# Pooled attention with a mixture of attention experts behind it, on one core: shared output chunks, another emission clock, another order of matmuls

## The chip, the cores and the metric

The kernel runs on one core of one Trainium2 chip. The metric is device time in microseconds (us), the median of several runs; lower is better. All numbers before the prediction come from runs and from one profiled execution of the kernel before the change.

## The reference

Two stages follow each other, in float32.

```python
# q, k, v: (8, 8, 1152, 64); the queries are averaged in pairs to 576
q_pool = q.reshape(B, H, S // 2, 2, D).mean(axis=3)
attn = softmax(q_pool @ k.T / sqrt(D));  x = attn @ v        # 8 heads -> x: (8, 576, 512)

logits = x @ w_gate                    # 4 experts, the best 2 of each token, softmax over those
for e in range(4):
    q, k, v = x @ wq[e], x @ wk[e], x @ wv[e]                # (8, 576, 64)
    a = softmax(causal(q @ k.T / sqrt(64)))
    out += gate[e] * (a @ v @ wo[e])                         # (8, 576, 512)
```

The maxima of the rows are subtracted before the exponential, so they are computed first. Inputs of `q`, `k`, `wq` and `wk` are large enough (x8) that the matmuls of the scores are done in split form, a high part and a low part.

## The kernel before, in words

**Tiles.** Heads go in pairs: 32 pairs, four to a batch, eight batches. A pair has its two heads in the two halves of the 128 partitions. Matmuls come in three shapes. Shape A (`rows2`, line 293) splits the array by rows, one half for each head: scores and the matmuls of the row maxima. Shape B (`cols2`, line 300) splits it by columns: products with `v` and the sums of the softmax's denominators. Shape C (`mm`, line 284) uses the whole array: projections, the output and small ones. PSUM is eight buffers of 512 columns (`gen`).

**Work of a pair.** `f_max` and `f_mxs` compute scores for the maxima, VectorE reduces them (`row_max`, line 540, into `PM`), and the maxima go as rows into `RM`. `f_st` computes the scores again, transposed and in split form (`qh`, `ql`, `kh`, `kl`, and a matmul with `RM` that subtracts the maximum); ACT takes the exponentials into `pt` (eleven buffers); `f_av` multiplies by `v`, and Pool (GpSimd) adds `pt` into `sacc` for the denominators (line 317). `f_xfin` normalises and splits the result into a high and a low part of `x`, in two ranges of queries, 256 and 320 (`g_split`, lines 707 to 716). The splitting of loaded inputs is done beside it: `f_prepq` adds the two halves of the queries on VectorE and forms `ql` (lines 471 and 483, both with two inputs in SBUF), `f_prepk` forms `kl` on Pool.

**Work of a batch's second stage.** Once four pairs are done, `f_qk` and `f_vproj` project `x`, `f_mmax` and `f_mst` do maxima and scores, `f_mask` masks on Pool, `f_mav` multiplies by `v`, and `f_yfin` leaves `y` (two head pairs of experts, high and low part, 576 tokens). `f_out` multiplies by `wo` in chunks of 128 tokens: five to a batch, the last of 64 tokens. A chunk is six matmuls of 512 columns (two pairs of experts; high by high, low by high, high by low), an ACT copy from PSUM and a store. The weights are split in `f_weights` early in the run (line 1084: VectorE subtracts, two inputs in SBUF). The work of a batch's second stage is laid between the pairs of the next.

**What sets the order.** Each piece of work is a generator (`Flow`). An emission loop (lines 1099 to 1120) keeps a clock for each engine (`clk`, `emit`): every emitted instruction adds a cost written in the code, waits in that clock for what it reads and writes, and adds 0.1 and 0.05 or 0.105 us where PE changes shape. The loop picks the next piece by those clocks, by priorities and by a table, `PLAN`, with a row of thirteen numbers for each of the 32 pairs and one for the tail. The numbers say, in order: how long PE may idle for a piece of the shape that it is in, in general, for scores and for products with `v`; how many waiting products make PE prefer shape B on leaving A; how many make it go there at all without a penalty of 3 us (`av_need`); how far the matmuls of the maxima may run ahead of VectorE; and priorities and lags of the maxima and of the second stage. So the costs and the table fix the order in which instructions are written on every engine; on the chip each engine runs its own list in that order, with semaphores between them.

**VectorE beside Pool.** In `dve_tt` (line 312) a cost of n / 960 + 0.069 us is charged for n elements. Only `any_tt`, which `f_prepq` uses, adds `PORT` = 0.38 us for Pool; the weights' subtraction adds nothing.

Of the kernel before, what the change touches and what calls it, by code (L numbers as in the profile page):

```python
# [7 lines left out]
F32 = mybir.dt.float32  # L8
# [41 lines left out]

PORT = 0.38

# [3 lines left out]

PLAN = [
# [33 lines left out]
]  # L91
INF = float("inf")
SEM = {"PE": 0.2, "ACT": 0.2, "DVE": 0.15, "POOL": 0.15, "SP": 0.0, "": 0.0}
# [58 lines left out]
def pooled_attention_then_moe_kernel(ctx: ExitStack, tc: tile.TileContext, qT, kT, vP, wall, wop, out):  # L152
# [80 lines left out]
    r_gs = ring("gs", [128, 2, 5, 4], F32, 2)  # L233
    r_y = ring("y", [128, 2, SQ], F32R, 2)
    r_ob = ring("ob", [128, DM], F32, 2)
# [5 lines left out]

    def emit(eng, cost, R=(), W=(), xfer=0.0, mode="C", late=0.0):
        t = clk[eng]
        if eng == "PE" and mode != cut[0]:

            t += DRAIN
            cost += LOAD[mode]
        for r in R:
            if r.we != eng:
                t = max(t, r.rw + late)  # L250
        for r in W:
            if r.ue != eng:
                t = max(t, r.ru)
        if eng == "PE":
# [12 lines left out]
        for r in W:  # L267
            if done >= r.w:
                r.w, r.we = done, eng
        return e  # L270
# [5 lines left out]

    def pe_cost(n):
        return max(0.11, n * 0.000455 + 0.002)

# [9 lines left out]
    def rows2(o, terms, R, W):  # L289

        for i, (l, r) in enumerate(terms):
            for j in range(2):
                nc.tensor.matmul(o(j), l(HEAD[j]), r(HEAD[j]), start=i == 0, stop=i == len(terms) - 1)  # L293
            n = o(0).shape[-1]
            emit("PE", pe_cost(n), R, W, 0.0, "A")

# [14 lines left out]

    def dve_tt(o, a, b, op, n, R, W, port=0.0):
        nc.vector.tensor_tensor(o, a, b, op=op)  # L313
        emit("DVE", n / 960 + 0.069 + port, R, W)

    def pool_tt(o, a, b, op, n, R, W):
        nc.gpsimd.tensor_tensor(o, a, b, op=op)  # L317
        emit("POOL", n * 0.0023 + 0.15, R, W)

    def any_tt(o, a, b, op, n, R, W):  # L320
        tail = prog["f"] > NP - 0.5
        e = max([clk["POOL"]] + [r.rw for r in R if r.we != "POOL"]) + n * 0.0023 + 0.06
        d = max([clk["DVE"]] + [r.rw for r in R if r.we != "DVE"]) + n / 960 + 0.069
        if e + (EET if tail else EE0 if prog["f"] == 0.0 else EES) < d:
            pool_tt(o, a, b, op, n, R, W)
        else:
            dve_tt(o, a, b, op, n, R, W, PORT)

# [28 lines left out]
    V, X, Y, VG, XR = {}, {}, {}, {}, {}  # L357
    VT, GT, GS, MT, YR = {}, {}, {}, {}, {}
    lows = {}
    prog = {"f": 0.0}  # L360

    def row(i):
        return PLAN[min(int(prog["f"] + 1e-6), NP)][i]

# [61 lines left out]
    def load_first():  # L426
# [7 lines left out]
        for t in range(3):  # L434
            kh = KH[0, t] = r_kh.new()
            act_copy(kh.ap, ks[t].ap, 384, [ks[t]], [kh], False)
            if t < 2:
                n = sl[t].stop - sl[t].start
                dve_tt(q[:, 0, sl[t]], q[:, 0, sl[t]], q[:, 1, sl[t]], ALU.add, n, [qs[t]], [qs[t]], 0.07)
                act_copy(qh[:, sl[t]], q[:, 0, sl[t]], n, [qs[t]], [QP[t]], False)  # L440
# [265 lines left out]

    def g_split(accs, den, n, hi, lo, res):

# [3 lines left out]
        yield lambda: rdy("ACT", den.rw)  # L712
        act_copy(hi, den[:, :n], n, [den], [res])
        yield lambda: rdy("DVE", res.rw)
        dve_tt(lo, den[:, :n], hi.bitcast(F32), ALU.subtract, n, [den, res], [res])
        den.free()

    def f_xfin(p, hf, acc, sacc):
# [5 lines left out]
        qc = slice(q0, q0 + qn)  # L724
        yield from g_split(accs, den, qn, x[:, 0, qc], x[:, 1, qc], xr)
        flag.add(("x", p, hf))
# [76 lines left out]
    def f_vproj(b, pt):  # L803
# [32 lines left out]
        def op(eng, f, *a, n=20, **kw):  # L836
            f(*a, **kw)
            emit(eng, 0.15 + n * 0.0023 if eng == "POOL" else 0.11 if eng == "ACT" else 0.25, [v32], [gate])

# [137 lines left out]
    def f_mask(b, ep, qb, c, pt, f, kn):  # L977
# [3 lines left out]
                                pattern=[[0, 2], [1, kn]], channel_multiplier=-1)  # L981
        emit("POOL", 0.38, [pt], [pt])
        spawn("mav", f_mav(b, ep, qb, c, pt), av_prio)
# [30 lines left out]
    def f_yfin(b, ep, qb, acc, sacc):  # L1014
# [9 lines left out]
        yr.u, yr.ue = y.u, y.ue  # L1024
        qc = slice(q0, q0 + qn)
        yield from g_split(accs, den, qn, y[:, 0, qc], y[:, 1, qc], yr)
        YR[b, ep, qb] = yr
# [10 lines left out]
    def f_out(b, ts, eps):  # L1038
        tail = b == NB - 1
        ro = r_pt if tail else r_ob  # L1040
        for t in ts:
            n = min(128, SQ - 128 * t)
            tk = slice(128 * t, 128 * t + n)
            yr = lambda ep: YR[b, ep, 0 if t < 2 else 1].rw if (b, ep, 0 if t < 2 else 1) in YR else INF
            yield (lambda: max(r_gen.avail(), ro.avail(), yr(eps[0]), 0.0 if tail else yr(eps[1])), "C")
            ps, ob = r_gen.new(), ro.new()
            o = ob.ap.rearrange("p a b -> p (a b)")[:, 0:DM] if tail else ob.ap
            for i, ep in enumerate(eps):
                if i and tail:
                    yield (lambda: yr(ep), "C")  # L1050
                y = Y[b, ep]
                for k, (yi, W) in enumerate(((0, OH), (1, OH), (0, OL))):
                    mm(ps[:n, :], y[:, yi, tk], W[:, ep, :], i + k == 0, i == 1 and k == 2, 0.233,
                       [YR[b, ep, 0 if t < 2 else 1]], [ps])
            m_prog[b] += 1.4
            act_copy(o[:n], ps[:n, :], DM, [ps], [ob])
            ps.free()
            mv(out[b * SQ + 128 * t:b * SQ + 128 * t + n, :], o[:n], [ob], [])
            ob.free()
        if not tail:  # L1060
            for ep in range(2):
# [5 lines left out]
    def f_weights():  # L1067
# [8 lines left out]
        for i, (hi, lo, src, n) in enumerate(parts):  # L1076
# [71 lines left out]
```

## Time and profile before

| what | value |
|---|---|
| median of 3 runs | 1207.52 us (1206.73 to 1207.64) |
| the profiled execution's own time | 1208.1 us |
| its span, first to last instruction | 1206.4 us |
| mean granted clock of TensorE | 0.993 |

How to read the rows below. PE is TensorE's matmuls, PEld its weight loads, DVE VectorE, ACT ScalarE, POOL GpSimd, SP the queue that issues DMAs. A row of groups gives line, engine, operation, output and inputs by the program's names, shapes, the number of instructions, then busy us and mean ns of one. A row of a timeline gives its start in us, its length in us (from the first start to the last end where several are merged, with their number after x), and in brackets the idle time of that engine before it with what ended it. A row of a stretch gives its bounds, its length, the busy time and instructions of PE, PEld, DVE, ACT and POOL, then the granted clock of TensorE (1.00 is 2.4 GHz, 0.50 is 1.2 GHz), the share of the DMA engines and GB/s. Matmuls are pipelined: consecutive ones overlap in the rows, and the pace is the distance of their starts.

### The profile page before, as it was taken

To read this page: it belongs to the slowest core of one execution; us is meant where nothing else is said; L and a number is where in the kernel's file an instruction comes from. 1 tells how busy PE (TensorE), PEld (TensorE's weight loads), DVE (VectorE), ACT (ScalarE), POOL (GpSimd) and SP (SyncE) were. 2 spreads that over 40 slices of the span, in tenths; PEclk is the share of its full clock that TensorE was granted. 3 is DMA by queue.
4 is the path that set the end of the run, shared out by engine and by line. 5 is a ranking of instruction groups with operands and counts; after the bars stand their busy time and mean duration, and the time that the engine had idled before them with its cause. 6 is when DMAs were issued, how large, how long until landed. Compare 5 with 4: busy or idle time off the path is not lost.

```text
span 1206.4 us, 29495 instructions
## 1 busy us (share of the span) xinstructions
PE 1164.3 (97%) x11257; PEld 902.1 (75%) x11257; DVE 861.6 (71%) x2073; ACT 703.5 (58%) x2024; POOL 973.6 (81%) x852
## 2 busy tenths in 40 slices
PE   6999999989999999999999999999999999999998
PEld 5666787767877778777886777877778777877775
DVE  7898667777677857777587776777667776677265
ACT  5656646645466654666646755566646765466534
POOL 4989998957789976999769987699786996889922
PEclk9989999989999999999999999999999999999999
DMA  5232222022210222113011221112311113200001
GB/s 157 74 93 78 67 61 60 9 79 74 61 54 15 82 71 61 54 53 108 16 51 54 63 93 32 42 54 69 98 41 47 35 63 97 60 22 2 20 22 41
DMA packets 40426, 70.32 MB, mean 58 GB/s; under 512 B 4870, under 2 KB 31452, under 8 KB 40284
## 3 DMA queue, kind: packets, MB, share of 16 engines
q1 hardware_dynamic: 40284, 68.43, 18.2%
q8 instruction: 89, 1.46, 0.5%
q14 instruction: 53, 0.43, 0.1%
HBM read 58.73 MB, written 9.44 MB: 57 GB/s over the span
## 4 chain that ended last, share of the span: by engine, by line
PE 78%; POOL 10%; DVE 8%; issue 2%; ACT 1%; DMA 0%; DVEq 0%; SPq 0%; POOLq 0%; ACTq 0%
PE gen L293 34%; PE gen L300 23%; PE gen L284 20%; POOL sacc L317 8%; DVE PM L540 2%; DVE gen L922 1%; DVE ql L313 1%; POOL kl L317 1%; ACT pt L634 1%; DVE gen L702 1%; DVE WL L313 1%; DVE rd L690 1%; DVE gen L313 1%; POOL pt L980 1%; PE gen L590 0%
## 5 line engine op out<-in xcount | busy, mean ns | idle before, releaser
L317 POOL TENSOR_TENSOR sacc<-sacc,pt 128x640 f32<-128x640 f32 (+2 forms) x588 | 828.1, 1414 | 141.1 <-ACT sacc L309 93.0
L540 DVE TENSOR_REDUCE PM<-gen 128x1 f32<-128x384 f32 x864 | 428.6, 549 | 186.2 <-PE gen L293 142.6
L634 ACT ACTIVATE pt<-gen 128x320 f32<-128x320 f32 (+1 forms) x1152 | 380.2, 433 | 150.0 <-PE gen L293 147.9
L300 PE MATMUL gen<-pt,v 128*64 128x320 f32 (+4 forms) x2752 | 356.1, 402 | 3.8 <-DVE MPM L922 2.1
L300 PEld LDWEIGHTS gen<-pt,v 128*64 128x64 f32 (+1 forms) x2752 | 195.7, 137 | 133.4 <-issue 11.5
L293 PE MATMUL gen<-qh,kh 64*128 64x320 f32 (+1 forms) x1152 | 207.3, 314 | 3.6 <-DVE PM L540 2.8
L293 PE MATMUL gen<-qh,kl 64*128 64x320 f32 (+1 forms) x1152 | 194.8, 298 | 0.0
L293 PE MATMUL gen<-ql,kh 64*128 64x320 f32 (+1 forms) x1152 | 190.2, 294 | 0.0
L293 PE MATMUL gen<-RM,ON 64*128 64x320 f32 (+1 forms) x1152 | 190.0, 293 | 0.0
L293 PE MATMUL gen<-kh,qh 64*128 64x384 f32 x768 | 157.2, 373 | 8.4 <-ACT qh L304 7.5
L293 PEld LDWEIGHTS gen<-qh,kh 64*128 64x128 f32 x1152 | 131.1, 187 | 34.2 <-issue 13.5
L293 PEld LDWEIGHTS gen<-RM,ON 64*128 64x128 f32 x1152 | 129.0, 188 | 0.0
L293 PEld LDWEIGHTS gen<-ql,kh 64*128 64x128 f32 x1152 | 128.7, 187 | 0.0
L293 PEld LDWEIGHTS gen<-qh,kl 64*128 64x128 f32 x1152 | 126.6, 187 | 0.0
L293 PEld LDWEIGHTS gen<-kh,qh 64*128 64x128 f32 x768 | 88.1, 188 | 38.6 <-issue 19.3
L284 PE MATMUL gen<-x,WH 128*128 128x320 f32 (+1 forms) x512 | 105.8, 301 | 7.6 <-DVE x L313 7.6
L317 POOL TENSOR_TENSOR kl<-kraw,kh 128x384 fp32r<-128x384 f32 x96 | 97.6, 1031 | 3.2 <-ACT kh L304 2.5
L284 PEld LDWEIGHTS gen<-x,WH 128*128 128x128 f32 x512 | 81.7, 188 | 11.9 <-issue 9.4
L922 DVE CUSTOM_DVE_ANT_0 gen<-gen,mqk 64x288 f32<-64x288 f32 (+4 forms) x160 | 74.4, 504 | 20.0 <-PE gen L293 17.2
L304 ACT CAST x<-gen 128x256 fp32r<-128x256 f32 x64 | 25.9, 404 | 89.5 <-DVE gen L313 89.5
L284 PE MATMUL gen<-x,WL 128*128 128x320 f32 (+1 forms) x256 | 75.5, 295 | 0.0
L962 ACT ACTIVATE pt<-gen 128x320 f32<-128x320 f32 (+2 forms) x224 | 63.7, 381 | 14.0 <-PE gen L293 12.8
(109 smaller groups left out, 1568.2 us busy)
## 6 DMA issues: line engine op xcount, KB each, us to landing
kraw<-in_kT SPq DMA_DIRECT2D x96, 192.0 KB
v<-in_vP SPq DMA_DIRECT2D x96, 192.0 KB
qraw<-in_qT SPq DMA_DIRECT2D x31, 576.0 KB
out<-ob SPq DMA_DIRECT2D x28, 256.0 KB
wst<-in_wall SPq DMA_DIRECT2D x8, 193.0 KB
out<-pt SPq DMA_DIRECT2D x4, 256.0 KB
RM<-nt SPq DMA_DIRECT2D x62, 2.5 KB
out<-ob SPq DMA_DIRECT2D x7, 128.0 KB
```

Source lines behind the costliest of these rows:

```text
L284: nc.tensor.matmul(o, lhsT, rhs, start=start, stop=stop)
L293: nc.tensor.matmul(o(j), l(HEAD[j]), r(HEAD[j]), start=i == 0, stop=i == len(terms) - 1)
L300: nc.tensor.matmul(o(HEAD[j]), l(j), r(j), start=start, stop=stop)
L304: nc.scalar.copy(o, i)
L313: nc.vector.tensor_tensor(o, a, b, op=op)
L317: nc.gpsimd.tensor_tensor(o, a, b, op=op)
L540: nc.vector.tensor_reduce(pm[:, i, t:t + 1], ps[:, :384], axis=AX.X, op=ALU.max)
L634: nc.scalar.activation(pts[i][:, j, :qn], st[j][:, qn * i:qn * i + qn], AF.Exp, scale=0.0625)
L690: nc.vector.transpose(rd[:, :n], den[:, :n])
L702: nc.vector.transpose(den[:, :n].rearrange("p (a b) -> p a b", b=32), r9[:, :k].unsqueeze(2).to_broadcast([128, k, 32]))
L922: nc.vector.tensor_tensor_reduce(p, p, mqk[:m, 384 + m - w:384 + m], 1.0, LOW, ALU.add, ALU.max, pm[:m, j, c, i:i + 1])
L962: nc.scalar.activation(pt_[:kn, j, f:qn], st[j][:kn, o - n:o], AF.Exp, scale=0.125)
```

## The change

Three things are edited. First, `y` holds 512 tokens of a batch, and the last 64 go into a tile of their own, `yl`, where the even batch has the first 64 columns and the odd batch the last 64; `f_out` of an even batch does four chunks, and that of an odd batch five, of which the fifth takes `yl` and is stored in two pieces. `g_split` takes a list of ranges instead of one. Second, the emission clock: `PORT` is 0.2 and is now added to Pool's clock, and a VectorE operation marked `port` waits in the clock for the end of the Pool instruction that runs when it would begin; Pool's instructions cost less if they follow an independent one without a gap; PE's costs are 1.8 times as high in the first 20 us; a few costs are finer. The weights' subtraction and what `any_tt` puts on VectorE are marked `port`. Third, `PLAN` has two rows for each pair, put together from a head of 16, a cycle of 8 that is repeated five times and a tail of 9.

```diff
-PORT = 0.38
+COLD = 20.0
+PORT = 0.2
+GR = 2
-PLAN = [
-    (0.15, 0.1, 0.1, 3, 4, 0.9, 0.02, 0.02, 3, 4.5, 2.9, 4.6, 4.55),
...
-    (0.1, 0.1, 0.3, 2, 4, 0.9, 0.3, -0.04, 1, 4.5, 2.9, 4.6, 4.55),
-    (0.1, 0.1, 0.3, 3, 4, 0.9, 0.3, 0.02, 1, 4.5, 3.9, 4.6, 4.75),
-    (0.1, 0.2, 0.1, 5, 1, 1.0, 0.08, 0.02, 1, 4.5, 3.9, 4.6, 4.75),
-    (0.1, 0.1, 0.3, 2, 4, 0.9, 0.3, -0.04, 1, 4.5, 2.9, 4.6, 4.55),
...
+CYCLE = [
+    (0.15, 0.1, 0.3, 1, 4, 0.9, 0.3, -0.02, 0, 4.5, 3.9, 4.6, 4.55),
+    (0.05, 0.1, 0.3, 4, 3, 0.9, 0.3, -0.02, 0, 4.5, 2.9, 4.6, 4.55),
+    (0.05, 0.1, 0.6, 5, 1, 1.0, 0.3, 0.02, 4, 4.5, 3.9, 4.6, 4.75),
+    (0.05, 0.1, 0.6, 5, 1, 1.0, 0.3, 0.02, 1, 4.5, 3.9, 4.05, 4.75),
+    (0.05, 0.1, 0.6, 4, 3, 1.0, 0.3, 0.04, 3, 4.5, 2.9, 4.6, 4.1),
+    (0.05, 0.1, 0.3, 4, 3, 0.9, 0.3, -0.02, 0, 4.5, 2.9, 4.6, 4.55),
+    (0.05, 0.45, 0.6, 4, 3, 1.0, 0.12, 0.04, 2, 4.5, 2.9, 4.6, 4.1),
+    (0.2, 0.45, 0.45, 4, 3, 1.0, 0.12, 0.04, 3, 4.5, 2.9, 4.6, 4.1),
+]
+PLAN = HEAD + CYCLE * 5 + TAIL
...
-    r_y = ring("y", [128, 2, SQ], F32R, 2)
+    r_y = ring("y", [128, 2, 512], F32R, 2)
+    r_yl = ring("yl", [128, 2, 2, 128], F32R, 1)
...
+        if eng == "PE" and t < COLD:
+            cost *= 1.8
+        if port:
+            i = len(held) - 1
+            while i >= 0 and held[i][0] > t:
+                i -= 1
+            if i >= 0 and held[i][1] > t:
+                t = held[i][1]
+            if clk["POOL"] > t:
+                clk["POOL"] += PORT
+        if eng == "POOL":
+            if t <= clk[eng] + 0.05 and not any(r in last[0] for r in (*R, *W)):
+                cost -= 0.115
+                held.append((t, t + cost))
+            else:
+                held.append((t, t + cost - 0.08))
...
-        return PLAN[min(int(prog["f"] + 1e-6), NP)][i]
+        return PLAN[min(int(prog["f"] * GR + 1e-6), NP * GR)][i]
...
         yield lambda: rdy("ACT", den.rw)
-        act_copy(hi, den[:, :n], n, [den], [res])
+        for a, k, hi, _ in outs:
+            act_copy(hi, den[:, a:a + k], k, [den], [res])
...
-            spawn("out", f_out(b, range(5), (0, 1)), m_prio(b, 3, "C"))
+            spawn("out", f_out(b, range(4 + b % 2), (0, 1)), m_prio(b, 3, "C"))
...
+                    l = YL[b // 2][:, ep, yi, :] if t == 4 else Y[b, ep][:, yi, 128 * t:128 * t + 128]
+                    mm(ps.ap, l, W[:, ep, :], i + k == 0, i == 1 and k == 2, 0.233, [YR[j, ep, q] for j in bs], [ps])
...
-            dve_tt(lo, w[:, :n], hi.bitcast(F32), ALU.subtract, n, [w, h], [wres])
+            dve_tt(lo, w[:, :n], hi.bitcast(F32), ALU.subtract, n, [w, h], [wres], True)
```

## Rows read from the trace of the kernel before

**Rows 1.** The page: span, busy time of each engine with its share of the span and its instructions, and the shares of the engines in the chain of work that ended last.

```profile
span 1206.4 us, 29495 instructions
PE 1164.3 (97%) x11257; PEld 902.1 (75%) x11257; DVE 861.6 (71%) x2073; ACT 703.5 (58%) x2024; POOL 973.6 (81%) x852
PE 78%; POOL 10%; DVE 8%; issue 2%; ACT 1%; DMA 0%; DVEq 0%; SPq 0%; POOLq 0%; ACTq 0%
```

**Rows 2.** Busy time by stretch, of a piece of the middle that is one batch long.

```profile
316.60:462.10 145.50, 142.94 (x1412) 112.11 (x1410) 105.48 (x253) 87.01 (x253) 122.53 (x107) 1.00 0.19 59
```

**Rows 3.** The waits of PE: who waited for whom, us in total, times, longest.

```profile
PE gen L284 <- DVE x L313: 7.6, 6, 1.4
...
PE gen L293 <- DVE PM L540: 3.2, 3, 1.7
```

**Rows 4.** The timeline from 600 to 614 us, all engines.

```profile
606.09 1.81 DVE L313 TENSOR_TENSOR ql<-qraw,qh 128x576 fp32r<-128x576 f32 x1
...
608.38 0.48 PE L284 MATMUL gen<-x,WH 128*128 128x256 f32 x2 [1.24 <-DVE x L313]
```

**Rows 5.** VectorE's subtractions of `ql` (of the instructions that touch the tile `ql`: minimum, median and maximum in ns, first and last start in us) and of the weights (the groups by line and shape).

```profile
L313 DVE TENSOR_TENSOR ql<-qraw,qh x31: 735/945/5574, 25.1 to 1080.5; 128x576 fp32r<-128x576 f32 x31
...
L313 DVE TENSOR_TENSOR WL<-wst,WH 128x386 fp32r<-128x386 f32 x8 | 11.2, 1412 | 0.0
```

**Rows 6.** Timelines of VectorE, PE and Pool around 60 and around 245 us.

```profile
58.67 3.22 DVE L313 TENSOR_TENSOR WL<-wst,WH 128x386 fp32r<-128x386 f32 x2
...
62.41 0.63 PE L293 MATMUL gen<-qh,kh 64*128 64x320 f32 x1 [1.72 <-DVE PM L540]
...
239.53 5.57 DVE L313 TENSOR_TENSOR ql<-qraw,qh 128x576 fp32r<-128x576 f32 x1 [1.95 <-PE gen L293]
...
241.03 1.95 POOL L317 TENSOR_TENSOR kl<-kraw,kh 128x384 fp32r<-128x384 f32 x2
...
242.94 8.41 POOL L317 TENSOR_TENSOR sacc<-sacc,pt 128x640 f32<-128x640 f32 x5
...
247.64 0.80 PE L284 MATMUL gen<-OH,y 128*128 128x512 f32 x1 [2.72 <-ACT y L304]
...
249.54 0.80 PE L284 MATMUL gen<-OH,y 128*128 128x512 f32 x1 [1.11 <-DVE y L313]
```

**Rows 7.** Busy time by stretch after those two places, and PE's timeline from 58 to 72 us.

```profile
62.50:69.00 6.50, 6.50 (x30) 3.94 (x32) 5.13 (x12) 2.74 (x7) 6.19 (x6) 0.50 0.11 33
...
250.00:253.00 3.00, 3.00 (x22) 2.35 (x23) 1.97 (x3) 0.72 (x2) 1.35 (x1) 0.50 0.26 92
...
66.38 0.47 PE L293 MATMUL gen<-ql,kh 64*128 64x320 f32 x2
66.64 0.47 PE L293 MATMUL gen<-RM,ON 64*128 64x320 f32 x2
...
70.16 0.31 PE L293 MATMUL gen<-qh,kl 64*128 64x320 f32 x2
70.30 0.31 PE L293 MATMUL gen<-ql,kh 64*128 64x320 f32 x2
```

**Rows 8.** The timeline from 1140 us, all engines: the last of three matmuls in two chunks of 128 tokens, and the same in a chunk of 64.

```profile
1143.36 0.40 PE L284 MATMUL gen<-OL,y 128*128 128x512 f32 x1
...
1144.06 0.40 PE L284 MATMUL gen<-OL,y 128*128 128x512 f32 x1
...
1149.00 0.40 PE L284 MATMUL gen<-OL,y 128*64 128x512 f32 x1
...
1149.69 0.40 PE L284 MATMUL gen<-OL,y 128*64 128x512 f32 x1
```

**Rows 9.** ACT's copies into `y` and a copy of 64 columns, from the groups by line and shape.

```profile
L304 ACT CAST QD<-qraw 64x64 fp32r<-64x64 f32 x64 | 15.7, 245 | 0.4
...
L304 ACT CAST y<-gen 128x320 fp32r<-128x320 f32 x16 | 6.8, 427 | 13.5 <-DVE gen L313 13.3
...
L304 ACT CAST y<-gen 128x256 fp32r<-128x256 f32 x16 | 6.2, 386 | 19.7 <-DVE gen L313 19.7
```

**Rows 10.** The end of the chain of work that ended last (start, us, what) and the timeline after 1202 us.

```profile
1198.01 4.33 PE gen L284 x17
...
1202.35 1.21 SPq L334 DMA_DIRECT2D out<-pt  x2
```

**Rows 11.** PE's timeline from 622 to 629 us, and from the page the group of the products with `v`.

```profile
622.66 0.34 PE L293 MATMUL gen<-kh,qh 64*128 64x384 f32 x2
622.84 0.29 PE L293 MATMUL gen<-qh,kh 64*128 64x256 f32 x2
...
623.32 0.41 PE L293 MATMUL gen<-kh,qh 64*128 64x384 f32 x2
623.93 0.76 PE L300 MATMUL gen<-sacc,ones 128*64 128x320 f32 x4 [0.20 <-ACT pt L634]
624.49 4.08 PE L300 MATMUL gen<-pt,v 128*64 128x256 f32 x36
628.50 0.44 PE L293 MATMUL gen<-kh,qh 64*128 64x384 f32 x2
628.78 0.31 PE L293 MATMUL gen<-qh,kh 64*128 64x320 f32 x2
...
L300 PE MATMUL gen<-pt,v 128*64 128x320 f32 (+4 forms) x2752 | 356.1, 402 | 3.8 <-DVE MPM L922 2.1
```

More of the change, by code (lines that the diff above doesn't have):

```diff
@@ L49 @@
 DRAIN, LOAD = 0.1, {"A": 0.105, "B": 0.05, "C": 0.105}
-PORT = 0.38
-PLAN = [
[33 rows of a table removed]
-]
+COLD = 20.0
+PORT = 0.2
+GR = 2
+HEAD = [
[16 rows of a table added]
+]
+CYCLE = [
[8 rows of a table added]
+]
+TAIL = [
[9 rows of a table added]
+]
+PLAN = HEAD + CYCLE * 5 + TAIL
 INF = float("inf")
@@ L240, in pooled_attention_then_moe_kernel, with emit @@
     cut = ["C"]
-    def emit(eng, cost, R=(), W=(), xfer=0.0, mode="C", late=0.0):
+    held, last = [(0.0, 0.0)], [()]
+    def emit(eng, cost, R=(), W=(), xfer=0.0, mode="C", late=0.0, port=False):
         t = clk[eng]
@@ L253, in emit @@
                 t = max(t, r.ru)
+        if eng == "PE" and t < COLD:
[14 more added lines that the diff above has]
+                held.append((t, t + cost - 0.08))
+            del held[:-12]
+            last[0] = W
         if eng == "PE":
@@ L275, in spawn, with pe_cost @@
             flows.append(f)
-    def pe_cost(n):
-        return max(0.11, n * 0.000455 + 0.002)
+    def pe_cost(n, m=128):
+        return max(0.00086 * m, n * 0.000455 + 0.002)
     def av_cost(n):
@@ L293, in rows2 @@
                 nc.tensor.matmul(o(j), l(HEAD[j]), r(HEAD[j]), start=i == 0, stop=i == len(terms) - 1)
-            n = o(0).shape[-1]
-            emit("PE", pe_cost(n), R, W, 0.0, "A")
+            m, n = o(0).shape
+            emit("PE", pe_cost(n, m), R, W, 0.0, "A")
     def cols2(o, l, r, start, stop, n, R, W):
@@ L310, in act_first, with dve_tt @@
         emit("ACT", n / 1200 + 0.083, R, W)
-    def dve_tt(o, a, b, op, n, R, W, port=0.0):
+    def dve_tt(o, a, b, op, n, R, W, port=False):
         nc.vector.tensor_tensor(o, a, b, op=op)
-        emit("DVE", n / 960 + 0.069 + port, R, W)
+        emit("DVE", n / 960 + 0.069, R, W, port=port)
     def pool_tt(o, a, b, op, n, R, W):
         nc.gpsimd.tensor_tensor(o, a, b, op=op)
-        emit("POOL", n * 0.0023 + 0.15, R, W)
+        emit("POOL", n * 0.0024 + 0.1, R, W)
     def any_tt(o, a, b, op, n, R, W):
         tail = prog["f"] > NP - 0.5
-        e = max([clk["POOL"]] + [r.rw for r in R if r.we != "POOL"]) + n * 0.0023 + 0.06
+        e = max([clk["POOL"]] + [r.rw for r in R if r.we != "POOL"]) + n * 0.0024 + 0.05
         d = max([clk["DVE"]] + [r.rw for r in R if r.we != "DVE"]) + n / 960 + 0.069
@@ L326, in any_tt @@
         else:
-            dve_tt(o, a, b, op, n, R, W, PORT)
+            dve_tt(o, a, b, op, n, R, W, True)
     def fl(ap):
@@ L357, in pooled_attention_then_moe_kernel @@
     V, X, Y, VG, XR = {}, {}, {}, {}, {}
-    VT, GT, GS, MT, YR = {}, {}, {}, {}, {}
+    VT, GT, GS, MT, YR, YL = {}, {}, {}, {}, {}, {}
     lows = {}
@@ L438, in load_first @@
                 n = sl[t].stop - sl[t].start
-                dve_tt(q[:, 0, sl[t]], q[:, 0, sl[t]], q[:, 1, sl[t]], ALU.add, n, [qs[t]], [qs[t]], 0.07)
+                dve_tt(q[:, 0, sl[t]], q[:, 0, sl[t]], q[:, 1, sl[t]], ALU.add, n, [qs[t]], [qs[t]])
                 act_copy(qh[:, sl[t]], q[:, 0, sl[t]], n, [qs[t]], [QP[t]], False)
@@ L705, in g_norm, with g_split @@
         box.extend((accs, den))
-    def g_split(accs, den, n, hi, lo, res):
+    def g_split(accs, den, n, outs, res):
         yield lambda: rdy("DVE", accs.rw)
@@ L712, in g_split @@
         yield lambda: rdy("ACT", den.rw)
-        act_copy(hi, den[:, :n], n, [den], [res])
+        for a, k, hi, _ in outs:
+            act_copy(hi, den[:, a:a + k], k, [den], [res])
         yield lambda: rdy("DVE", res.rw)
-        dve_tt(lo, den[:, :n], hi.bitcast(F32), ALU.subtract, n, [den, res], [res])
+        for a, k, hi, lo in outs:
+            dve_tt(lo, den[:, a:a + k], hi.bitcast(F32), ALU.subtract, k, [den, res], [res])
         den.free()
@@ L724, in f_xfin @@
         qc = slice(q0, q0 + qn)
-        yield from g_split(accs, den, qn, x[:, 0, qc], x[:, 1, qc], xr)
+        yield from g_split(accs, den, qn, [(0, qn, x[:, 0, qc], x[:, 1, qc])], xr)
         flag.add(("x", p, hf))
@@ L837, in op @@
             f(*a, **kw)
-            emit(eng, 0.15 + n * 0.0023 if eng == "POOL" else 0.11 if eng == "ACT" else 0.25, [v32], [gate])
+            emit(eng, 0.25 + n * 0.0023 if eng == "POOL" else 0.11 if eng == "ACT" else 0.25, [v32], [gate])
         PL, pl = ("DVE", nc.vector) if b == NB - 1 else ("POOL", nc.gpsimd)
@@ L981, in f_mask @@
                                 pattern=[[0, 2], [1, kn]], channel_multiplier=-1)
-        emit("POOL", 0.38, [pt], [pt])
+        emit("POOL", 0.15 + 0.0025 * kn, [pt], [pt])
         spawn("mav", f_mav(b, ep, qb, c, pt), av_prio)
@@ L1024, in f_yfin @@
         yr.u, yr.ue = y.u, y.ue
-        qc = slice(q0, q0 + qn)
-        yield from g_split(accs, den, qn, y[:, 0, qc], y[:, 1, qc], yr)
+        k = min(qn, 512 - q0)
+        outs = [(0, k, y[:, 0, q0:q0 + k], y[:, 1, q0:q0 + k])]
+        if k < qn:
+            if b // 2 not in YL:
+                yield lambda: 0.0 if b // 2 in YL else r_yl.avail()
+                if b // 2 not in YL:
+                    YL[b // 2] = r_yl.new()
+            yl, o = YL[b // 2], 64 * (b % 2)
+            yr.u, yr.ue = max((yr.u, yr.ue), (yl.u, yl.ue))
+            outs.append((k, 64, yl[:, ep, 0, o:o + 64], yl[:, ep, 1, o:o + 64]))
+        yield from g_split(accs, den, qn, outs, yr)
         YR[b, ep, qb] = yr
@@ L1041, in f_out @@
         for t in ts:
-            n = min(128, SQ - 128 * t)
-            tk = slice(128 * t, 128 * t + n)
-            yr = lambda ep: YR[b, ep, 0 if t < 2 else 1].rw if (b, ep, 0 if t < 2 else 1) in YR else INF
+            q = 0 if t < 2 else 1
+            bs = (b - 1, b) if t == 4 else (b,)
+            yr = lambda ep: max(YR[i, ep, q].rw for i in bs) if all((i, ep, q) in YR for i in bs) else INF
             yield (lambda: max(r_gen.avail(), ro.avail(), yr(eps[0]), 0.0 if tail else yr(eps[1])), "C")
@@ L1050, in f_out @@
                     yield (lambda: yr(ep), "C")
-                y = Y[b, ep]
                 for k, (yi, W) in enumerate(((0, OH), (1, OH), (0, OL))):
-                    mm(ps[:n, :], y[:, yi, tk], W[:, ep, :], i + k == 0, i == 1 and k == 2, 0.233,
-                       [YR[b, ep, 0 if t < 2 else 1]], [ps])
+                    l = YL[b // 2][:, ep, yi, :] if t == 4 else Y[b, ep][:, yi, 128 * t:128 * t + 128]
+                    mm(ps.ap, l, W[:, ep, :], i + k == 0, i == 1 and k == 2, 0.233, [YR[j, ep, q] for j in bs], [ps])
             m_prog[b] += 1.4
-            act_copy(o[:n], ps[:n, :], DM, [ps], [ob])
+            act_copy(o, ps.ap, DM, [ps], [ob])
             ps.free()
-            mv(out[b * SQ + 128 * t:b * SQ + 128 * t + n, :], o[:n], [ob], [])
+            for i, j in enumerate(bs):
+                n = 128 // len(bs)
+                mv(out[j * SQ + 128 * t:j * SQ + 128 * t + n, :], o[n * i:n * i + n], [ob], [])
             ob.free()
+        if 4 in ts:
+            yl = YL.pop(b // 2)
+            yl.u, yl.ue = max((YR[j, ep, 1].u, YR[j, ep, 1].ue) for ep in range(2) for j in (b - 1, b))
+            yl.free()
         if not tail:
```

53 rows, old and new, of tables (CYCLE, HEAD, PLAN, TAIL) are left out of this document.

## The prediction

> **What bounds the kernel now.** I read the page's busy times and its chain first. TensorE (PE) is busy 1164.3 of 1206.4 us, and the chain that ended last runs 78% through it [rows 1]. GpSimd (Pool) is busy 81% of the span, yet holds only 10% of the chain. Then I cut the middle of the run into pieces of one batch's length: in such a piece of 145.5 us PE is busy 142.94 us at the full granted clock [rows 2]. So work taken from PE is worth nearly its length, and idle PE is some 2.6 us of a batch. A busy PE is not yet one that streams, though: it also pays when it changes from one shape of matmul to another, which I price below.
>
> Next I asked who ends PE's idle time. VectorE's second half of `x` ends 7.6 us in six waits, its row maxima 3.2 us in three [rows 3]. The timeline shows the mechanism for the first: at 606.09 VectorE begins the subtraction of `ql`, which takes 1.81 us; the half of `x` stands behind it in VectorE's queue, and PE idles 1.24 us before the first matmul that needs it [rows 4]. The same subtraction took 0.735 us at best, 0.945 in the median and 5.574 at worst; the one of the weights, two thirds as long in elements, takes 1.412 us in the mean [rows 5]. The emission clock of the kernel before prices the first at 576/960 + 0.069 + 0.38 = 1.05 us and the second at 386/960 + 0.069 = 0.47 us, with nothing for Pool. PE's order is written for a VectorE that is ahead of the real one.
>
> Two places early in the run show what that does at worst. Two subtractions of weights fill 3.22 us from 58.67, and PE then waits 1.72 us for a row maximum. At 239.53 a subtraction of `ql` lasts 5.57 us, while Pool goes through two `kl` and into the next sums; PE then stands 2.72 and 1.11 us before output matmuls that want `y` [rows 6]. After both, the granted clock is 0.50 of full speed, which is 1.2 GHz [rows 7].
>
> **The change part by part.**
>
> *Output chunks.* Before, every batch has five output chunks of six 512-column matmuls, the fifth of 64 tokens. After, an even batch has four, and the fifth of the odd one holds the last 64 tokens of both. That removes 4 x 6 = 24 matmuls. Three matmuls of a 128-token chunk start 0.70 us apart as a group, three of a 64-token chunk 0.69 [rows 8]: the price is one of columns, and the chunk filled to 128 tokens costs no more. 24 x 0.69 / 3 = 5.5 us come off PE. Four ACT copies go too, on an engine that is busy 58%; nothing for that. DMAs stay as many, since a shared chunk is stored in two pieces. Bounds: 0, if PE only waits longer at these places for something else; 5.5 us, if the queue moves up. In a batch where PE idles under 2%, I take 5.5.
>
> *The split of `y`.* The last 320 tokens of a head pair are now written as 256 and 64, into two tiles. An ACT copy of 320 columns takes 427 ns, of 256 columns 386, and a small one of 64 columns 245 [rows 9], so one becomes two of 0.63 us, 0.2 us more; VectorE's subtraction splits alike, for about as much. This happens 16 times and is hidden behind PE's other work everywhere but in the last batch. There the last `y` releases 17 output matmuls that run without a break to the end, and two stores follow [rows 10]. Nothing covers the split there, so 0.4 us, and the last chunk now issues two stores instead of one; two issues fill 1.21 us of SP's queue, 0.6 us each, of which I take 0.5. I add 0.9 us, between 0.2 (other pieces hide the split and the store) and 1.5.
>
> *The `yl` tile.* It has one buffer, which an even batch takes and the next odd batch's output frees. The next taker comes most of a batch later (145 us, rows 2), so the new wait for it is hidden; if output fell a whole batch behind, `y` itself would hold things up as well.
>
> *The clocks.* They issue nothing: they only change which order is written. VectorE's two-input operations in SBUF now wait for the Pool instruction that runs when they begin, the weights' subtractions as well, and Pool's own costs are finer. What this can win is what a wrong clock cost. Waits for `x`, 7.6; the 1.72 after the weights, and the rest of the 3.2 for maxima, 3.2 in all; for `y` 2.72 + 1.11 = 3.8: together 14.6 us [rows 3, 6]. The clock comes on top. From 62.5 to 69 PE ran at 1.2 GHz; pairs of matmuls start 0.26 us apart there and 0.14 at 2.4 GHz [rows 7], so 6.5 us did the work of 3.5: 3.0 lost. From 250 to 253, busy all through at 1.2 GHz, 3.0 x 0.46 = 1.4 lost. The ceiling is 14.6 + 4.4 = 19.0 us; the floor is 0, if the new order meets as many late VectorE operations elsewhere. I take 10 us, near the middle: for the waits of the `x` kind, the weights' stall and its low clock (7.6 + 1.7 + 3.0 = 12.3 us) the late operation was held for about one Pool instruction, which the new clock sees; the hold at 239.53 it would see only for its first Pool instruction; and an order that avoids these waits will have some of its own.
>
> The Trainium skill's page "SBUF — State Buffer" (section "SBUF: two separate sides") says that the pair of ports is locked by whichever operation starts first, for that whole instruction, and the other blocks. The 1.81 us of rows 4 agree with it. The 5.57 us of rows 6 don't: VectorE was held past several Pool instructions, so the measurement decides. By that rule alone the new clock would be right and the gain nearer the 19.0. By rows 6 it stays partly blind, which is the first rival below.
>
> *The order.* 33 rows of one pair each become 65 of half a pair, eight of them repeated for the middle batches. What is late next can't be read from a trace of the old order, but the price of one unit can. Going from row-shape matmuls to column-shape ones: 623.32 to 623.93 is 0.61 us, less the pair's own 0.18 (622.66 to 622.84) and 0.20 idle, 0.23; and back, 628.50 to 628.78 less 0.18, 0.10 [rows 11]. A visit to the column shape costs 0.33 us. The one shown holds 40 matmuls; 2752 for `v` alone [rows 11] would be 69 visits of that length, so there are some 70 or more. A tenth fewer or more is 2.3 us. I take 0, with 8 us either way (a third).
>
> **The sum.** -5.5 + 0.9 - 10 + 0 = -14.6. The profiled execution took 1208.1 us around a span of 1206.4; the median of the runs is 1207.5, 0.6 less, and I set the sum against it: 1207.5 - 14.6 = 1193 us, 1186 to 1199 by the spread of the waits and the order.
>
> **The rivals.**
>
> *Only the chunks count* (1203 us). The waits move to other places, since VectorE must still wait for Pool and is held past several instructions at times. 1207.5 - 5.5 + 0.9 = 1202.9. For it: the hold of rows 6; the six waits for `x` are over 0.6% of the span only together. Against: the wait of rows 4 is a plain misprice.
>
> *All of it goes* (1183 us). The whole 19.0, with low clock: 1207.5 - 5.5 + 0.9 - 19.0 = 1183.9, and a few visits fewer. For it: the new rows accept up to 0.6 us of idle PE rather than leave the column shape. Against: PE idles at other places too, and no order removes every wait.
>
> *Shorter visits* (1216 us). In the repeated rows PE may go to the column shape with three or even one product waiting, where most rows before wanted four. If visits get half as long, there are 70 more: 70 x 0.33 = 23.1, and -14.6 + 23.1 = +8.5. It decides from 14.6 / 0.33 = 44 more visits, six in ten. The skill's page "TensorEngine Tiling (Array Packing)", section "Key Properties", says a change of tiling mode drains the engine; the 0.23 and 0.10 us of rows 11 agree. Against: the preference on leaving the row shape asks for four or five waiting products now.
>
> *The change doesn't do what it says* (1207 us): the order starves PE at the start of the run or in the last batch, with one more stretch at 1.2 GHz like that of rows 7 (1.7 + 3.0 us) and a wait or two of the same size, and that eats the chunks and what is saved elsewhere.
>
> **How the numbers follow.** Under 0.2% (2.4 us) a measurement of this kernel can't tell a change from none. Forecast 0.45, only the chunks 0.20, all of it 0.18, shorter visits 0.11, no effect 0.06. Faster: 0.45 + 0.20 + 0.18 = 0.83, less 0.01 for the edge, 0.82; same 0.07; slower 0.11. The range leaves out half of "all of it" below and "shorter visits" above: 1181 to 1208.
>
> **What would show it.** Right: 24 fewer output matmuls and none with 64 tokens; PE's wait for `x` under 3 us in all; subtractions of `ql` still over 1.5 us, but with PE at work beside them; no stretch at 1.2 GHz near 62 or 247; a batch in the middle of under 144.5 us. Wrong: a middle batch that is only 0.7 us shorter (the chunks alone), more changes of shape in it, or a new stretch at half clock.

## The result, and the profile after

The kernel after takes 1215.9 us in the median of four runs (1215.55 to 1216.46), beside 1207.6 us for the kernel before on the same chip: a ratio of 1.0069, 95% interval 1.0052 to 1.0086. It is slower by 8.3 us, where 1193 us was forecast.

The page of the kernel after: span, busy times, and the chain that ended last, by engine and by line.

```profile
span 1213.8 us, 29441 instructions
PE 1160.3 (96%) x11233; PEld 893.0 (74%) x11233; DVE 877.6 (72%) x2091; ACT 703.8 (58%) x2036; POOL 971.6 (80%) x850
PE 57%; POOL 29%; DVE 8%; issue 2%; ACT 2%; DMA 0%; POOLq 0%; SPq 0%; DVEq 0%; ACTq 0%
POOL sacc L349 25%; PE gen L325 23%; PE gen L316 17%; PE gen L332 16%; DVE qraw L345 3%; POOL kl L349 3%; POOL pt L1014 2%; DVE PM L572 1%; DVE gen L956 1%; ACT pt L666 1%; DVE ql L345 1%; PE gen L622 0%; DMA qraw<-in_qT 0%; DVE gen L734 0%
```

The 24 matmuls are gone (11257 to 11233, against [rows 1]) and PE is busy 4 us less, yet the span is 7.4 us longer: PE idles 11 us more. Pool's share of the chain went from 10 to 29%, though Pool itself is busy no longer than before. VectorE is busy 16 us longer with practically the same work. That is the first sign: an engine that is "busy" longer on the same instructions is being held.

The waits of PE after (who waited for whom, us in total, times, longest).

```profile
PE gen L332 <- POOL sacc L349: 14.0, 18, 1.6
PE gen L325 <- DVE PM L572: 10.9, 5, 2.2
...
PE gen L316 <- DVE x L345: 6.8, 6, 1.2
```

Two lines are new in size: 14.0 us for Pool's sums and 10.9 us, in five waits of 2.2, for row maxima. The wait for `x` is almost what it was (7.6 in [rows 3]).

The instructions that touch the tile `qraw`: minimum, median and maximum in ns, first and last start.

```profile
L345 DVE TENSOR_TENSOR qraw<-qraw x33: 426/935/6748, 5.4 to 1059.4; 128x576 f32<-128x576 f32 x31, 128x320 f32<-128x320 f32 x1, 128x256 f32<-128x256 f32 x1
```

This is the sum of the two query halves, which VectorE does once for each pair. Its maximum was 2146 ns in the kernel before; here it is 6748, and five of the 31 take that long: at 389.42, 538.15, 686.85, 835.50 and 984.27 us, once in each batch for which the repeated rows of the new table write the order. The timeline at the first of them, of VectorE, then Pool, then PE:

```profile
389.42 6.74 DVE L345 TENSOR_TENSOR qraw<-qraw 128x576 f32<-128x576 f32 x1
396.09 1.94 DVE L572 TENSOR_REDUCE PM<-gen 128x1 f32<-128x384 f32 x4
...
389.01 4.63 POOL L349 TENSOR_TENSOR sacc<-sacc,pt 128x640 f32<-128x640 f32 x3
393.59 1.01 POOL L349 TENSOR_TENSOR kl<-kraw,kh 128x384 fp32r<-128x384 f32 x1
394.55 1.92 POOL L349 TENSOR_TENSOR sacc<-sacc,pt 128x384 f32<-128x384 f32 x2
...
394.07 0.44 PE L325 MATMUL gen<-kh,qh 64*128 64x384 f32 x2
396.69 0.39 PE L325 MATMUL gen<-qh,kh 64*128 64x256 f32 x2 [2.18 <-DVE PM L572]
```

An operation of this size takes 0.74 us at its best (`ql`, [rows 5]). The sum begins while Pool is in the first of three `sacc`, and stays through those, a `kl` and the first of two more `sacc`. Pool takes each of these without a pause from the one before (the record of one ends no earlier than that of the next begins). The second `sacc` of the last pair reads what the first wrote and starts only 0.08 us after it ends (395.550 and 395.628 us in the records of single instructions). VectorE is done at 396.17, which is 0.62 us after that pause began. The other four long sums end 0.62 us after the same place in Pool's list. Four row maxima stand behind the sum in VectorE's queue, and PE waits 2.18 us for them.

Behind two of the five waits the granted clock falls too. Busy time by stretch (the last three columns are the granted clock, the DMAs' share and GB/s): two pieces right behind the second and the fourth, and a piece one batch long.

```profile
546.30:549.70 3.40, 3.40 (x24) 2.14 (x20) 1.89 (x4) 2.63 (x8) 0.27 (x1) 0.50 0.45 140
...
843.20:846.60 3.40, 3.40 (x28) 2.67 (x26) 1.92 (x4) 2.64 (x10) 0.00 (x0) 0.51 0.42 135
320.00:468.70 148.70, 142.84 (x1408) 110.53 (x1408) 109.80 (x253) 87.48 (x254) 121.57 (x106) 1.00 0.19 59
```

After the waits that end at 545.41 and at 842.76 the granted clock is 0.50, that is 1.2 GHz, for 3.4 us. The same work, from the first of these matmuls to the first of the next group of scores, takes 9.21 us there (545.41 to 554.62) and 7.63 us behind the wait that ends at 694.12, where the clock stayed at 2.4 GHz (to 701.75): 1.6 us each time. A batch takes 148.7 us; one before took 145.5 [rows 2]. Where each pair's last scores end says the same by stages: at the ninth pair the new kernel is 8.8 us ahead (303.5 against 312.3 us), at the 29th it is 9.1 us behind (1047.1 against 1038.0). So the new order is 8.8 us ahead when the repeated rows begin, and loses 17.9 in the five batches that they govern.

### The profile page after: what moved, and what is told of

Its sections match the earlier page's. It is cut to its first block, busy times and chain, and to the rows that moved or that the text cites. A ratio compares the mean times of both kernels' runs of the same rounds, so it can differ in the third digit from the quotient of the medians.

```text
span 1213.8 us, 29441 instructions
## 1 busy us (share of the span) xinstructions
PE 1160.3 (96%) x11233; PEld 893.0 (74%) x11233; DVE 877.6 (72%) x2091; ACT 703.8 (58%) x2036; POOL 971.6 (80%) x850
## 4 chain that ended last, share of the span: by engine, by line
PE 57%; POOL 29%; DVE 8%; issue 2%; ACT 2%; DMA 0%; POOLq 0%; SPq 0%; DVEq 0%; ACTq 0%
POOL sacc L349 25%; PE gen L325 23%; PE gen L316 17%; PE gen L332 16%; DVE qraw L345 3%; POOL kl L349 3%; POOL pt L1014 2%; DVE PM L572 1%; DVE gen L956 1%; ACT pt L666 1%; DVE ql L345 1%; PE gen L622 0%; DMA qraw<-in_qT 0%; DVE gen L734 0%; DVE gen L345 0%
## 5 line engine op out<-in xcount | busy, mean ns | idle before, releaser
L349 POOL TENSOR_TENSOR sacc<-sacc,pt 128x640 f32<-128x640 f32 (+4 forms) x586 | 824.8, 1412 | 138.2 <-ACT sacc L341 101.8
L332 PEld LDWEIGHTS gen<-pt,v 128*64 128x64 f32 (+1 forms) x2752 | 191.7, 137 | 136.8 <-issue 11.3
L325 PE MATMUL gen<-qh,kh 64*128 64x320 f32 (+1 forms) x1152 | 211.4, 317 | 13.4 <-DVE PM L572 10.9
L332 PE MATMUL gen<-sacc,ones 128*64 128x320 f32 (+1 forms) x384 | 66.7, 428 | 14.5 <-POOL sacc L349 14.0
L722 DVE STREAM_TRANSPOSE rd<-gen 128x256 f32<-128x256 f32 (+1 forms) x96 | 45.6, 475 | 41.3 <-PE gen L332 40.8
```

The costliest lines, as they stand in the source:

```text
L332: nc.tensor.matmul(o(HEAD[j]), l(j), r(j), start=start, stop=stop)
L722: nc.vector.transpose(rd[:, :n], den[:, :n])
```

## The experiments

**Theory 1:** VectorE gets past Pool only at a pause between two Pool instructions; the new order puts five sums into long runs without one, and that costs the time. **Theory 2:** the sums are only a symptom; Pool is late in the new repeated order (14.0 us of waits for `sacc`, 25% of the chain), and this costs the time. Medians of the kernel before in the four batches of runs lie between 1206.8 and 1207.6 us, so differences of medians between kernels of different batches are good to about 0.8 us.

### The chunks alone

The kernel before with shared chunks, the split of `y` and the `yl` tile; table and clock stay.

```diff
-            spawn("out", f_out(b, range(5), (0, 1)), m_prio(b, 3, "C"))
+            spawn("out", f_out(b, range(4 + b % 2), (0, 1)), m_prio(b, 3, "C"))
```

> The kernel before with the shared output chunks alone: old table, old emission clock. Theory 1 (in the repeated rows VectorE's sum of the query halves is held 6.7 us behind a run of Pool instructions, and PE idles 2.2 us a batch for it) and theory 2 (in the repeated rows Pool's sums come late for the denominators: PE waits 14.0 us for them, 3.3 before) both put the loss in the order, so the chunks alone should give about 1203 us (1207.6 - 5.5 + 0.9). Theory 3 (the shared chunks cost what they save, by the split of y and the fixed pairing of batches): 1207 us or more.

Measured: 1209.6 us (1205.64 to 1210.34, ten runs), ratio 1.0011 (1.0000 to 1.0021). A miss. The time lands in the branch of a third theory, that the chunks cost what they save; the run with 24 matmuls put back, below, speaks against that. The ten runs fall into two groups: four at 1205.6 to 1207.3 us with a mean granted clock of 0.997, six at 1209.4 to 1210.3 with 0.994 to 0.996, so the median is good to some 4 us only. 24 matmuls fewer give little or nothing by themselves here. An edit of the work also moves the emission clock, and the order changes with it: Pool's list, which the edit doesn't touch, differs from its 427th instruction on. That this ate the gain is likely, and not shown. Price and order have to be parted in another way (the last experiment but one).

### New clock with the old table, and old rows in the repeated part

Two kernels: chunks and new clock with the 33 rows of before; and the kernel after with the old rows, each twice, for pairs 8 to 27.

```diff
-PLAN = HEAD + CYCLE * 5 + TAIL
+PLAN = HEAD + [r for r in MID for _ in range(2)] + TAIL
```

> Chunks and the new emission clock, but the old table of 33 rows. If the clock alone is worth what I forecast for it, 1193 to 1198 us. If the clock is neutral and the new table is what lost (theories 1 and 2), about 1203 us like the chunks alone. If the clock itself misleads the order, 1208 us or more.

> The changed kernel with its head and tail rows, but the middle (pairs 8 to 27) with the old rows, each twice. In the trace of after the head is 8.8 us ahead of before at the end of the eighth pair and 9.1 us behind at the end of the 28th: the repeated rows lose 17.9 us in five batches. Theories 1 and 2: the loss goes, 1198 to 1203 us. Theory 3, or a loss that comes from the new clock in any table: above 1208 us.

Measured: 1272.2 us (ratio 1.0533, 1.0517 to 1.0548) and 1226.6 us (1.0156, 1.0141 to 1.0171). Both miss what theories 1 and 2 let expect, and land in the open branch that was written for a clock that misleads in any table (above 1208 us). That reading is not the only one: a table is fitted to the clock it was written with. The 33 rows that give 1207 us with the old clock, and 1209.6 with the old clock and shared chunks, give 1272 with the new one; and the new clock with its own rows gives 1196.9 us once the sums are changed (next experiment). Neither kernel tells the theories apart.

### All 31 sums as a reduction of one input

The order of instructions on every engine stays that of the kernel after. Only the instruction of the sum changes: VectorE adds the halves as a reduction over them (one input, into a tile of its own, `qsum`) instead of an addition of two inputs; what read the sum reads `qsum`. `NM` goes into the first columns of `MRM[0]`, to make room.

```diff
-        any_tt(q[:, 0, :], q[:, 0, :], q[:, 1, :], ALU.add, SQ, [q], [q])
+        qs = r_qs.new(); nc.vector.tensor_reduce(qs.ap, q.ap.rearrange("p a n -> p n a"), axis=AX.X, op=ALU.add); emit("DVE", SQ / 960 + 0.069, [q], [q], port=True)
```

> The changed kernel in exactly its own order of instructions on every engine, but VectorE sums the two query halves with a reduction over one input in place of an addition with two (into a tile of its own, 1152 elements read, an estimated 1.2 us at 1152 / 960). It should then not be held by Pool. Theory 1: the 6.7 us operations become about 1.3 us, PE's 2.2 us waits go, and the time falls by 11 us (five waits) to 18 us (all that the repeated rows lost): 1198 to 1205 us. Theory 2: the operation gets short and the waits for Pool's sums stay, 1212 to 1217 us.

Measured: 1196.9 us (1196.56 to 1197.56), ratio 0.9914 (0.9897 to 0.9930): 19.0 us below the kernel after, and faster than both kernels, and 1 us below the range of theory 1. The sums in it, and the waits of PE:

```profile
L503 DVE TENSOR_REDUCE qsum<-qraw x31: 1366/1385/1401, 17.1 to 1040.4; 128x576 f32<-128x1152 f32 x31
```

```profile
PE gen L332 <- POOL sacc L349: 7.2, 10, 1.0
...
PE gen L316 <- DVE x L345: 6.8, 6, 1.2
...
PE gen L325 <- DVE PM L572: 0.6, 1, 0.6
```

The reduction takes nearly twice the 0.74 us of an undisturbed addition, but the same every time: none is held, in the places where the addition took 6.74 us. The 10.9 us for row maxima are 0.6, and the waits for `sacc` fall by half, without any edit to Pool. Busy time in a piece one batch long shows what a batch takes now, 145.2 us against 148.7:

```profile
320.00:465.20 145.20, 142.01 (x1400) 110.53 (x1398) 104.30 (x251) 87.17 (x253) 120.28 (x106) 1.00 0.19 59
```

PE's busy time in it is 0.8 us less than in the longer piece (142.01 against 142.84), so 2.7 of the 3.5 us are idle PE.

### The reduction in five pairs only

As before, but only pairs 13, 17, 21, 25 and 29 reduce; the other 26 add two inputs.

```diff
+        nc.vector.tensor_reduce(...) if p in (13, 17, 21, 25, 29) else nc.vector.tensor_tensor(qs.ap, q[:, 0, :], q[:, 1, :], op=ALU.add)
```

> The changed kernel in its own order, with the one-input reduction for five of the 31 sums of query halves alone: pairs 13, 17, 21, 25 and 29, whose sums lasted 6.74 us each in the trace of after. If these five holds are the loss (theory 1), nearly all of the gain of the run with all 31 reductions comes: 1197 to 1200 us. If holds in general cost, not these, under half of the gain: 1207 us or more.

Measured: 1200.5 us (1199.52 to 1200.9), ratio 0.9948 (0.9933 to 0.9963). That is 0.5 us above the range of theory 1 and far below the other. Five instructions carry 15.4 of the 19.0 us. From the eighth to the 28th pair, the five batches of the repeated rows, the run takes 14.9 us less than the kernel after (722.9 against 737.8), and neither stretch at 1.2 GHz behind the waits is left (one of 3.4 us stands at 111.5 us instead). Its waits for Pool, beside a 1.5 us wait for `kl`:

```profile
PE gen L332 <- POOL sacc L349: 13.2, 16, 1.6
```

They stand nearly where they stood (14.0 in the kernel after), with 15 us gone from the time. So theory 2 falls as the cause of these 15 us. The other 3.6 us go with the 26 other sums; the waits for `sacc` fall from 13.2 to 7.2 us with them, and no run parts the two.

### A pause in Pool's queue

The kernel after with its two-input sums. Pool gets two tiny instructions where each sum is emitted, the second reading what the first writes, so that a pause stands in its queue there.

```diff
+        nc.gpsimd.memset(scr[:, 0:1], 0.0)
+        nc.gpsimd.tensor_tensor(scr[:, 1:2], scr[:, 0:1], scr[:, 0:1], op=ALU.add)
```

> The changed kernel with its two-input sums, but with two tiny Pool instructions (1 element each, the second waits for the first) put into Pool's queue where each sum is emitted. Theory 1 with its mechanism, that VectorE gets in only where Pool pauses between one instruction and a dependent next one: the five 6.74 us sums end at the pause in the middle of the run, at 2 to 4 us, PE's waits of 2.18 us for the maxima go, and the time falls to 1198 to 1206 us in spite of some 10 us more on Pool. If VectorE is held for another reason (a count of instructions, a priority), the sums stay near 6.7 us and the time at 1214 to 1220.

Measured: 1204.5 us (1203.75 to 1204.81, ten runs), ratio 0.9981 (0.9972 to 0.9990). The same place in its timeline, VectorE and then Pool:

```profile
389.99 4.84 DVE L346 TENSOR_TENSOR qraw<-qraw 128x576 f32<-128x576 f32 x1
...
389.59 4.62 POOL L350 TENSOR_TENSOR sacc<-sacc,pt 128x640 f32<-128x640 f32 x3
394.15 0.09 POOL L504 MEMSET scr<- 1x1 f32 x1
394.32 0.55 POOL L505 TENSOR_TENSOR scr<-scr 1x1 f32<-1x1 f32 x1
394.84 0.99 POOL L350 TENSOR_TENSOR kl<-kraw,kh 128x384 fp32r<-128x384 f32 x1
```

The sum ends at 394.83. Until then it was held past two boundaries without a pause (at 391.13 and 392.64 us). The pause that was put in stands between 394.24 and 394.32, and the sum ends 0.59 us after it begins. But it also ends 0.62 us after the last `sacc` (at 394.21 in the records of single instructions), where the memset comes next, and 0.62 is the distance in the kernel after. So VectorE may have got in ahead of the memset, which writes one element and reads nothing, and not at the pause behind it; no run parts the two. The sums last 4.84 us, longer than the 2 to 4 us expected. PE's wait for row maxima falls from 10.9 to 1.3 us:

```profile
PE gen L326 <- DVE PM L575: 1.3, 5, 0.3
```

11.4 us come back for two added instructions per pair on an engine that is busy 80% of the time. PE's waits for Pool hardly change: 11.2 us for `sacc` and 2.9 for the new instructions, beside 14.0 for `sacc` in the kernel after. This is theory 1 from the other side: VectorE's instruction is untouched, only Pool's list is. It shows that the length of the hold costs the time; it doesn't show that a pause is what ends it.

### The order of before, with reductions

```diff
-        any_tt(q[:, 0, :], q[:, 0, :], q[:, 1, :], ALU.add, SQ, [q], [q])
+        qs = r_qs.new(); nc.vector.tensor_reduce(...)
```

> The kernel before in its own order, with all 31 sums as one-input reductions. Its sums lasted 0.74 to 2.15 us, 42.5 us in all, and the reduction takes 1.39 each, 43 in all. Theory 1 says that the form itself is worth nothing here: 1204 to 1209 us. If the reduction helps in any order (say by leaving Pool undisturbed), about 1197 us, as it did for the order of after.

Measured: 1202.7 us (1201.71 to 1203.49), ratio 0.9967 (0.9956 to 0.9978). Below the range expected (1204 to 1209), and far from 1197: the two-input sums cost the kernel before about 4 us too. Its trace is 2.8 us ahead by the end of the second pair (71.0 against 73.8 us), where the stretch at 1.2 GHz of [rows 7] near 62 us is gone. With both orders free of them, the chunks and the new order are worth 5.8 us together (1202.7 to 1196.9).

### The chunks' price, in one order

The kernel with all reductions, in which each even batch issues the six matmuls of its fourth chunk a second time, over the same result: 24 more, in the same order of everything else.

```diff
+            if t == 3 and b % 2 == 0:
+                for i, ep in enumerate(eps):
+                    for k, (yi, W) in enumerate(((0, OH), (1, OH), (0, OL))):
+                        nc.tensor.matmul(ps.ap, Y[b, ep][:, yi, 384:512], W[:, ep, :], start=i + k == 0, stop=i == 1 and k == 2)
```

> The kernel with the 31 reductions in the order of after, and in each even batch the six matmuls of the fourth output chunk are issued twice, so 24 matmuls of 512 columns come back in nearly the places where the change took them away. If the shared chunks are worth PE's time, 5.5 us more than without: 1202.4 us (24 x 0.23). If PE waits at these places for something else anyway, 1197 to 1199 us.

Measured: 1202.0 us (1201.81 to 1202.58), ratio 0.9962 (0.9947 to 0.9977): 5.1 us for 24 matmuls, a hit. What is left for the new order and clock, with the sums out of the way, is 1202.7 - 1202.0 = 0.7 us, less than the measurement can tell from nothing.

### A clock that sees the whole run

The kernel after, and the one with all reductions, with a clock that prices a held VectorE operation to the end of the whole run of Pool instructions without a pause.

```diff
-            if i >= 0 and held[i][1] > t:
-                t = held[i][1]
+            while 0 <= i < len(held) and held[i][0] <= t + 0.01 and held[i][1] > t:
+                t, i = held[i][1], i + 1
```

> The kernel after, with one edit in the emission clock: a VectorE operation that must wait for Pool is priced to the end of the whole run of Pool instructions that follow each other without a pause, not to the end of the first of them. Same table; the order is written anew by it. If the clock's short price is what puts the sums into long runs, the planner now sees 5 to 7 us there and either moves them or builds PE's order around them: no wait of PE for a row maximum of 2.2 us is left, and if the table still fits, the time falls from 1215.9 to 1198-1208 us. If the table was fitted to the short price, the new order has other faults: the 2.2 us waits are gone, but the time stays at 1212 or more, as two re-planned kernels before it did. If the price doesn't matter to where the sums go, five sums of 6.7 us and the waits stay, with 1214-1217 us.

> The kernel with all 31 sums as reductions, with the same edit in the clock; now only the subtractions (ql, y, x, weights) and the other two-input operations are repriced. What is left to win there are the six waits for x behind a ql of 1.8 us (6.8 us in all) and the sums' waits for Pool (7.2 us). If the longer price helps, 1190-1196 us; if the order by this table was as good as it gets, 1196-1205 us.

Measured: 1237.3 us (ratio 1.0249, 1.0232 to 1.0267) and 1235.3 us (1.0229, 1.0214 to 1.0244). The sums of the first of them:

```profile
L345 DVE TENSOR_TENSOR qraw<-qraw x33: 426/965/2104, 5.3 to 1071.1; 128x576 f32<-128x576 f32 x31, 128x320 f32<-128x320 f32 x1, 128x256 f32<-128x256 f32 x1
```

No sum is held long any more (2.1 us at most), which fits a price that ended too soon as what let the five into the runs; as the whole order is another one, it is no proof. And the time rises by 21 us: the order is written anew, one `ql` is now held 6.4 us, and 14.6 us are lost up to the eighth pair alone (283.4 against 268.8 us). The second kernel is 38 us slower than without the edit, outside both branches that were written for it. A better clock with rows fitted to a worse one is no better kernel.

## Why the prediction was wrong

**The chunks: right.** 5.5 us were forecast from columns; 5.1 were measured in one order. In the time of the kernel before with chunks alone they can't be seen, as the order moves with them.

**The tail: about right.** From the start of ACT's last copy into `y` to the end it was 7.2 us before and is 7.8 now, 0.6 more against the 0.9 forecast. The prediction misread one thing: the 17 matmuls of [rows 10] begin at 1198.01, ahead of the last copy at 1199.21, so it wasn't the last `y` that released them, and PE didn't wait for that copy. After the change it does, for 0.40 us. The copies before and after, and the wait:

```profile
1199.21 0.43 ACT L304 CAST y<-gen 128x320 fp32r<-128x320 f32 x1 [2.06 <-DVE gen L313]
```

```profile
1206.03 0.37 ACT L336 CAST y<-gen 128x256 fp32r<-128x256 f32 x1 [2.35 <-DVE gen L345]
...
1206.45 1.07 PE L316 MATMUL gen<-OH,y 128*128 128x512 f32 x2 [0.40 <-ACT y L336]
```

**The clocks: the step that failed.** The term was -10 us, in the bounds -19 to 0, "the floor is 0, if the new order meets as many late VectorE operations elsewhere". It was about +15: 19.0 us for two-input sums in the new order, less 4.1 that they cost the old one. With -5.1 for the chunks and -0.7 for the rest of order and clock that makes 9.1, where 8.3 was measured. The prediction had the mechanism in hand, the 5.57 us of [rows 6], and wrote that the new clock would see such a hold "only for its first Pool instruction". It then counted this as a gain missed, and its floor of 0 let the new order meet as many late operations as before, not more. It met more: five sums were held 6.74 us where the longest sum in the kernel before took 2.15, once for each repeat of the rows. That they came to stand there because the clock priced the hold too low is argued; the run with the longer price agrees with it and doesn't prove it. What they cost is shown by the run that reduces these five alone: 15.4 us, of which 5 x 2.18 us of waits and two stretches at 1.2 GHz of 1.6 us each are 14.1.

Page and measurement differ here as they did in the prediction. The Trainium skill, "SBUF — State Buffer", section "SBUF: two separate sides", lets the one that starts first keep the ports for the whole instruction while the other blocks. The runs show more: 6.74 us past four boundaries between Pool instructions, to the end of the fifth. The same section names operations with two SBUF inputs among those that contend, with a GpSimd operation that reads SBUF; there the trace agrees, with 31 reductions of one input at 1366 to 1401 ns beside the same Pool work.

**The order: right in the sum, not in its parts.** 0 was taken, 8 us either way, as a guess about what couldn't be read. With the sums out of the way it is 0.7 us to the good. Beneath that, with reductions in both, the head of the run gains (302.0 against 309.7 us at the ninth pair), and the repeated rows give some of it back: from the ninth to the 29th pair 145.2 us a batch, where the old rows take 144.6 without the shared chunks.

**The waits for `x`: not removed.** 7.6 us became 6.8, behind a `ql` that still takes up to 2.0 us. "Under 3 us" was wrong. The stretches at 1.2 GHz near 62 and 247 us are gone as forecast; two new ones came.

**The rivals.** "Shorter visits" gave 1216 us, which is the time that came, and it is refuted: by a count of the recorded matmuls by line, PE visits the column shape 98 times, before 107, and changes between the three shapes 329 times, before 372. The number agrees by accident. "Only the chunks count" had the right mechanism, a hold past several Pool instructions, and the wrong bound: it let the waits move, not grow. "The change doesn't do what it says" came nearest in kind, but looked for the fault at the start and in the last batch; it was in the rows that repeat.

What stays open: what lets a held VectorE operation in at one boundary between Pool instructions and not at another (last section); where the last 3.6 of the 19.0 us come from; and how a table fitted to a clock that sees whole runs would do. That takes a search of the table, which wasn't tried.

## What to carry to other kernels

Where an order is written by a planner, an error in a price needn't be neutral: ask where the planner may put work because the price is too low, and bound that as a loss, times the number of repeats. A table fitted to one clock need not hold under another, so test the parts of such a change with the order held fixed: change one instruction's form, not the plan. And when VectorE shares its time with a Pool that is 80% busy, an operation that takes twice as long but is never held (here a reduction of one input) can be worth 19 us.

## What was not expected of the hardware

A two-input VectorE operation in SBUF can stay held past several Pool instructions, if these follow each other without a pause. When it gets in, it does so at the end of a Pool instruction: in the records of single instructions of all twelve traces, the 335 sums and `ql` of 128x576 that took over 1.0 us end 0.61 to 0.62 us after the end of one. None of them was held past a pause (mostly 0.08 us, between a Pool instruction and one that needs its result). In the kernel after, 23 of 26 got in at a pause, and the five long sums were held past 20 boundaries without one. But a pause isn't the only door: the other three, at 80.13, 203.14 and 240.02 us, got in at a boundary where Pool's records overlap by 0.04 to 0.05 us, and in the kernel before nine of 40 did, against five such boundaries that were passed. So theory 1 is too strong in its word "only"; what tells the boundaries apart is open. Two tiny instructions on Pool gave back 11.4 us. And the five waits of 2.2 us by PE were followed by the 1.2 GHz level in two cases only, at 546.3 and 843.2 us.
